# Where dS is turned and multiplied in an attention backward: fewer turns on TensorE, more products on GpSimd, dQ one group later

## The chip, the cores and the metric

The kernel runs on one core of a Trainium2 chip. The metric is the device time of one execution in microseconds, the median of several runs. PE is the matrix engine (TensorE), ACT is ScalarE, DVE is VectorE, POOL is GpSimd and SP is SyncE, which here issues DMAs.

## The reference

The program is a transformer block with adaptive layer norm, forward and backward: it returns the block's output and the gradients of nine inputs. The sequence has 2048 rows, the model 512 columns, and the attention 32 heads of 16 columns each.

```
h = layernorm(x) * (1 + ca) + sa                    # sa, ca, ga, sb, cb, gb from silu(c) @ w_mod
q, k, v = split(h @ wqkv)                           # 32 heads of 16
p = softmax(q k^T / 4);  o = p v
x = x + ga * (o @ wo)
h = layernorm(x) * (1 + cb) + sb
out = x + gb * (relu(h @ w1 + b1)^2 @ w2 + b2)
# and the vector-Jacobian product of all this with grad_out
```

The change is in the backward of the attention. For each head, with all 2048 x 2048 scores computed once more, it forms

```
P  = exp(scale * q k^T)            # row sums are folded into dO
dP = dO v^T - rowsum terms         # the terms ride along as two more rows of dO and v
dS = dP * P
dK = dS^T q;  dV = P^T dO;  dQ = dS k
```

## The kernel before

The forward takes the first part of the execution; it ends with the gradients of the feed-forward weights. Then `attn_bwd` works through 16 pairs of heads (`g`, `jp`). A pair is cut into 4 chunks `c` of 512 keys, and a chunk into 4 groups of 4 query blocks `ib` of 128 rows. A group is thus 4 blocks x 2 heads `a` = 8 tiles of 128 queries x 512 keys. I number the groups of a pair m = 0 to 15 (m = 4c + ib // 4). There are 256 groups in all.

For each tile, in the order in which the loop writes the instructions, PE computes the scores `st` (L1586), ACT takes the exponential into `pu` (L1589), and one block later PE computes `dp` (L1511, in `dP`) and DVE multiplies it with `pu` into the group's tile `ds` (L1515). Each engine runs its instructions in the written order. The PSUM tiles `st` and `dp` have three buffers each, `pu` has six, `ds` three, `dsT` four. The st and dp products use different halves of the array's rows and run side by side.

In groups with odd m (`off` is true), the second head's tile of the block i = 1 goes another way: ACT copies `dp` from PSUM to one of two SBUF tiles, `junk6` or `csq` (L1523, in `dP_pool`), and GpSimd multiplies it with `pu` (L1524). DVE has 7 products in such a group, and 8 in one with even m.

dK and dV come from `ds` and `pu` as they are (`kv`, L1455: four products side by side in four column strips of the array). `kv_two` takes two waiting units after every second block; in odd groups it takes them one at a time, at two places. dQ needs dS with the keys on the partitions. For this the group's `ds` tile, 32 blocks of 128 x 128, is transposed into `dsT` by a DMA that SP issues once a group (L1532, in `dS`), when the group's last product has been written. In groups with even m, `turn_ds` lets PE turn the first four of the blocks (L1545) into an `st` buffer, ACT copies them to `dsT` (L1546), and the DMA transposes the remaining 28. Then `dq` forms dQ (L1478) from `dsT` and the keys. Its calls wait in the list `pendq`, eight for each group; the loop takes four at every even block while more than 4 x 4 are waiting, which is to say two groups.

When a pair ends, `kvT` (filled by an ACT copy at the end of each chunk, L1458) is turned on PE and copied by ACT to `dk_t` and `dv_t` in two halves (`turn`, L1468 and L1472), and `dqT` (a DVE copy of the sums, L1483) is turned once (`turn_q`, L1491 and L1492). These three wait in `turnq`, and one is taken at block i = 3 of each group.

Loads for the next pair are cut in pieces and spread over the groups. Each is issued from GpSimd's queue (L1575) behind a copy of one element of `ds` into `tick` (L1574), which holds the load back until the group before is done.

Of the kernel before, what the change touches and what calls it, by code (L numbers as in the profile page):

```python
# [105 lines left out]
class K:  # L106
# [1322 lines left out]
    def attn_bwd(self):  # L1429
# [8 lines left out]
        S, D, H, NQ, ST, SC = self.S, self.D, self.H, self.NQ, self.ST, self.SC  # L1438
        G = 4
# [7 lines left out]
        pend, pendq, turnq = [], [], []  # L1447

        def kv(u):
            (T, g, jp, c, ib, kvT, pu, ds) = u  # L1450
            for j, (n, src) in enumerate((("Q", ds), ("dO", pu))):
                for a in range(2):
                    r = 64 * j + 32 * a
                    col = (2 * jp + a) * DH
                    nc.tensor.matmul(acckv[r:r + DH, :], lhsT=T[n][:, ib, col:col + DH], rhs=src[:, a, :],  # L1455
                                     start=(ib == 0), stop=(ib == ST - 1))
            if ib == ST - 1:
                nc.scalar.activation(kvT[:, 512 * c:512 * (c + 1)], acckv[:], ACT.Copy, scale=kvs[:])  # L1458

        def turn(g, jp, kvT, s0):  # L1460

            if kvT is None:
                return turn_q(g, jp)
            h0 = 4 * g + 2 * jp
            n = ST // 2
            tp = stp.tile([P, n, P], BF16, name="st")
            for st in range(n):
                nc.tensor.transpose(tp[:, st, :], kvT[:, (s0 + st) * P:(s0 + st + 1) * P], self.ident[:])  # L1468
            v = tp[:].rearrange("p s (t a e) -> p t s a e", t=2, a=2)
            for t, dst in enumerate((self.dk_t, self.dv_t)):  # L1470
                d = dst[:, s0:s0 + n, h0 * DH:(h0 + 2) * DH].rearrange("p s (a d) -> p s a d", a=2)
                nc.scalar.copy(d, v[:, t, :, :, 0:DH])  # L1472
# [21 lines left out]
        def kv_two(n=2):  # L1494
            for _ in range(n):
                u = pend.pop(0)
                kv(u)
                (T, g, jp, c, ib, kvT, pu, ds) = u
                if ib < ST - 1:
                    continue  # L1500
                if c % 2 and (g, jp) == (NQ - 1, 1):
                    turnq.append((g, jp, kvT, 4 * (c - 1)))
                elif c == SC - 1:
                    turnq.extend((g, jp, kvT, s0) for s0 in (0, ST // 2))

        def dP(u, a):

            (T, g, jp, c, ib, kvT, pu, dsg, i, grp) = u
            rd = slice(64 - 64 * jp, 128 - 64 * jp)
            dp = dpp.tile([P, 512], F32, name="dp")  # L1510
            nc.tensor.matmul(dp[:], lhsT=T["dOT"][rd, ib * P:(ib + 1) * P],  # L1511
                             rhs=masked["VT"][a][rd, 512 * c:512 * (c + 1)], start=True, stop=True)
            if a == 1 and i == 1 and off(c, ib):
                return dp
            nc.vector.tensor_tensor(dsg[:, i, a], dp[:], pu[:, a, :], ALU.mult)  # L1515

        def off(c, ib):
            return (c * SC + ib // G) % 2 == 1

        def dP_pool(u, dp):  # L1520
            (T, g, jp, c, ib, kvT, pu, dsg, i, grp) = u
            f = (self.junk6, self.csq)[(c * SC + ib // G) // 2 % 2]
            nc.scalar.copy(f[:], dp[:])  # L1523
            nc.gpsimd.tensor_tensor(dsg[:, i, 1], f[:], pu[:, 1, :], ALU.mult)  # L1524

        def dS(u):

            (T, g, jp, c, ib, kvT, pu, dsg, i, grp) = u
            pend.append((T, g, jp, c, ib, kvT, pu, dsg[:, i]))
            if i == G - 1:  # L1530
                dsT, n = grp
                nc.sync.dma_start_transpose(dsT[:, n:, :], dsg[:].rearrange("p i a k -> p (i a k)")[:, n * P:])  # L1532
                for a in range(2):
                    for sub in range(4):
                        pendq.append((T, g, jp, c, ib - G + 1, a, sub, dsT))

        def turn_ds(dsg, grp, skip):

            dsT = dtp.tile([P, 8 * G, P], BF16, name="dsT")
            grp.extend((dsT, 0 if skip else 4))  # L1540
            if skip:
                return
            tp = stp.tile([P, 4, P], BF16, name="st")
            for b in range(4):
                nc.tensor.transpose(tp[:, b, :], dsg[:, 0, 0, b * P:(b + 1) * P], self.ident[:])  # L1545
            nc.scalar.copy(dsT[:, 0:4, :], tp[:])  # L1546
# [4 lines left out]
        for g in range(NQ):  # L1551
            for jp in range(2):
                if jp == 0:
                    if g + 1 < NQ:
                        Tn, later = self.load_group(g + 1)
                    else:
                        Tn, later = None, self.wq_pieces(1) + self.load_wmt()
                    cut = len(later) // 2 if Tn else len(later)
                    pieces = self.pair_pieces(g, 1) + later[:cut]
                    later = later[cut:]  # L1560
                elif g + 1 < NQ:
                    pieces = self.pair_pieces(g + 1, 0) + later
                else:
                    pieces = [(self.xhat1_6[:, st, :], self.xhat1_d.rearrange("(st p) d -> p st d", p=P)[:, st, :])
                              for st in range(ST)]
                kvT = kvp.tile([P, S], BF16, name="kvT")
                total = len(pieces)
                for c in range(SC):
                    c0 = 512 * c
                    for ib0 in range(0, ST, G):  # L1570
                        m = c * (ST // G) + ib0 // G
                        while pieces and (total - len(pieces)) * SC * ST <= m * G * total:
                            if last:
                                nc.gpsimd.tensor_copy(tick[:], last[7][0:1, 0, 0, 0:1])  # L1574
                            nc.gpsimd.dma_start(*pieces.pop(0))  # L1575
                        dsg, grp = self.dsp.tile([P, G, 2, 512], BF16, name="ds"), []
                        for i in range(G):
                            ib = ib0 + i
                            q = slice(ib * P, (ib + 1) * P)
                            if turnq and i == 3:  # L1580
                                turn(*turnq.pop(0))
                            pu = self.pup.tile([P, 2, 512], BF16, name="pu")
                            for a in range(2):
                                stt = stp.tile([P, 512], F32, name="st")
                                rs = slice(64 * jp, 64 * jp + 64)
                                nc.tensor.matmul(stt[:], lhsT=T["QT"][rs, q], rhs=masked["KT"][a][rs, c0:c0 + 512],  # L1586
                                                 start=True, stop=True)
                                held = dP(last, a) if last else None
                                nc.scalar.activation(pu[:, a, :], stt[:], ACT.Exp, scale=self.scale)  # L1589
                                if held is not None:  # L1590
                                    dP_pool(last, held)
                                if a == 0 and i % 2 == 1 and off(c, ib) and len(pend) >= 4:
                                    kv_two(1)
                            if last:
                                dS(last)
                            last = (T, g, jp, c, ib, kvT, pu, dsg, i, grp)
                            if i % 2 == 1 and len(pend) >= 4:
                                kv_two(1 if off(c, ib) else 2)
                            elif i % 2 == 0 and len(pendq) > 4 * G:
                                for _ in range(8 if len(pendq) > 6 * G else 4):  # L1600
                                    dq(pendq.pop(0))
                            if i == 2:
                                turn_ds(dsg, grp, off(c, ib))
            T = Tn
        with tc.manual_schedule(engines=ALL):
            for t in (2, 0):
# [339 lines left out]
```

## Time and profile before

| | |
|---|---|
| Median of 3 runs | 2515.72 us (2510.71 to 2517.65) |
| The profiled execution | 2515.11 us, of which the span from the first to the last instruction is 2513.3 us |
| Granted TensorE clock, mean | 0.998 |
| Busy, share of the span | PE 97%, PEld 45%, DVE 68%, ACT 91%, POOL 28% |
| First and last exponential of the backward | 1166.5 and 2387.7 us |
| DMA transposes of dS | 256; 5.3 / 6.9 / 9.7 us from issue to landing (least, median, most) |
| Queue of these transposes | 71.5% of the time of 16 DMA engines |

The profile is of one execution. A line of its groups gives the source line, engine and operation, out<-in by the program's names, the shapes and the count, then the busy time and the mean duration of one in ns, then the idle time of the engine before these instructions and what ended most of it. Durations of neighbouring instructions on one engine overlap, so the distance between two starts is often less than the duration.

### The profile page before, as it was taken

What the parts mean: (1) busy time and instruction counts of PE and PEld (TensorE: products, weight loads), DVE (VectorE), ACT (ScalarE), POOL (GpSimd) and SP (SyncE); (2) the same over time, 40 slices, a digit from 0 to 9 for tenths busy, and PEclk for the clock granted to TensorE, in tenths of its full rate; (3) what the DMA queues carried; (4) which work ended last, traced back from release to release, by engine and by line L of the source; (5) the groups of instructions that cost most, each with busy time, mean ns of one, the idle gap of its engine ahead of it and who ended that gap; (6) DMA issues with size and microseconds to landing.
All of it is one profiled execution on the core that took longest, in us unless ns stands there. A gap on an engine that the chain in (4) does not pass through costs nothing.

```text
span 2513.3 us, 76903 instructions
## 1 busy us (share of the span) xinstructions
PE 2437.6 (97%) x30791; PEld 1133.6 (45%) x30791; DVE 1708.5 (68%) x3519; ACT 2297.0 (91%) x3773; POOL 715.9 (28%) x1289
## 2 busy tenths in 40 slices
PE   8999999999999999999999999999999999999998
PEld 4555555555555554673333333333333333333343
DVE  6222323422332333677999999999999999999957
ACT  7999999999999997535999999999999999999935
POOL 2344531321131022255222222222222222222223
PEclk9999999999999999999999999999999999999999
DMA  4589661441343044699999999999999999999997
GB/s 166 135 180 206 173 117 67 112 100 45 102 118 75 24 134 134 133 203 210 233 225 218 219 228 221 228 227 219 221 221 226 227 224 219 227 224 231 237 191 205
DMA packets 1260558, 446.30 MB, mean 178 GB/s; under 512 B 1204052, under 2 KB 1228246, under 8 KB 1260198
## 3 DMA queue, kind: packets, MB, share of 16 engines
q1 hardware_dynamic: 1219654, 336.29, 71.5%
q0 software_dynamic: 38464, 104.04, 13.7%
q8 instruction: 241, 3.95, 0.6%
q10 hardware_dynamic: 2080, 1.05, 0.1%
q14 instruction: 119, 0.97, 0.1%
HBM read 75.83 MB, written 64.49 MB: 56 GB/s over the span
## 4 chain that ended last, share of the span: by engine, by line
PE 55%; ACT 24%; DMA 12%; issue 4%; DVE 3%; POOL 0%; SPq 0%; DVEq 0%; ACTq 0%; POOLq 0%
ACT pu L391 19%; PE st L1586 15%; DMA dsT<-ds 10%; PE st L388 8%; PE acckv L1455 7%; PE accq L1478 5%; ACT pu L1589 4%; PE accbank L322 3%; DVE ds L1515 2%; PE dps L1050 2%; PE pps L1237 2%; PE dp L1511 1%; PE st L1545 1%; PE dps L995 1%; PE pps L631 1%
## 5 line engine op out<-in xcount | busy, mean ns | idle before, releaser
L1515 DVE TENSOR_TENSOR ds<-dp,pu 128x512 bf16<-128x512 f32 x1920 | 1180.5, 684 | 33.2 <-PE dp L1511 26.4
L1589 ACT ACTIVATE pu<-st 128x512 bf16<-128x512 f32 x2048 | 1075.3, 657 | 34.6 <-PE st L1586 21.3
L391 ACT ACTIVATE pu<-st 128x1024 bf16<-128x1024 f32 x992 | 912.1, 1077 | 2.9 <-PE st L388 2.7
L388 PE MATMUL st<-QTm,KTq 128*128 128x512 bf16 x1984 | 587.7, 377 | 19.5 <-ACT pu L391 6.0
L322 PEld LDWEIGHTS <-pu 128*128 128x128 bf16 x8192 | 347.5, 96 | 235.7 <-issue 2.5
L1511 PE MATMUL dp<-kvm,q 64*128 64x512 bf16 x1024 | 363.5, 384 | 1.3 <-DVE g2w L1056 0.7
L1511 PE MATMUL dp<-kvm,dOTg 64*128 64x512 bf16 x1024 | 362.2, 384 | 0.0
L322 PE MATMUL accbank<-Vaug,pu 128*128 128x17 bf16 x8192 | 357.7, 171 | 1.2 <-ACT Vaug L522 0.9
L1586 PE MATMUL st<-kvm,q 64*128 64x512 bf16 x1024 | 349.9, 381 | 4.7 <-ACT pu L1589 0.2
L1586 PE MATMUL st<-kvm,QTg 64*128 64x512 bf16 x1024 | 349.4, 381 | 4.0
L388 PEld LDWEIGHTS <-KTq 128*128 128x128 bf16 x1984 | 188.1, 96 | 176.1 <-issue 124.4
L1524 POOL TENSOR_TENSOR ds<-junk,pu 128x512 bf16<-128x512 f32 x64 | 73.9, 1154 | 370.3 <-ACT junk L1523 284.1
L1455 PE MATMUL acckv<-ds,Qg 128*16 128x512 bf16 x1024 | 176.2, 382 | 0.0
L1455 PE MATMUL acckv<-pu,dOg 128*16 128x512 bf16 x1024 | 175.9, 382 | 0.0
L1455 PE MATMUL acckv<-pu,q 128*16 128x512 bf16 x1024 | 175.8, 382 | 0.0
L1455 PE MATMUL acckv<-ds,q 128*16 128x512 bf16 x1024 | 175.8, 382 | 0.0
L1524 POOL TENSOR_TENSOR ds<-csq,pu 128x512 bf16<-128x512 f32 x64 | 73.8, 1153 | 354.5 <-ACT csq L1523 354.5
L302 POOL DMA_DIRECT2D QTm<-QTq_d x124 | 63.3, 512 | 340.8 <-PE st L388 320.0
L1586 PEld LDWEIGHTS <-q 64*128 64x128 bf16 x1024 | 66.9, 93 | 141.0 <-issue 108.8
L1586 PEld LDWEIGHTS <-QTg 64*128 64x128 bf16 x1024 | 66.6, 93 | 141.0 <-issue 108.0
L329 DVE RECIPROCAL rl<-accbank 128x4 f32<-128x4 f32 x128 | 23.0, 179 | 157.4 <-PE accbank L322 157.2
L1478 PE MATMUL accq<-dsT,Kg 128*32 128x128 bf16 x4096 | 105.5, 221 | 10.5 <-DMA dsT<-ds 10.2
(387 smaller groups left out, 3168.2 us busy)
## 6 DMA issues: line engine op xcount, KB each, us to landing
KTq<-KTq_d POOLq DMA_DIRECT2D x24, 512.0 KB, 3.7
duT_d<-auT POOLq DMA_DIRECT2D x3, 1792.0 KB, 7.7
aT_d<-rT POOLq DMA_DIRECT2D x3, 1792.0 KB, 11.1
KTq_d<-KTq SPq DMA_DIRECT2D x32, 128.0 KB, 2.2
QTq_d<-ev_fm SPq DMA_DIRECT2D x32, 128.0 KB, 4.3
ktm_d<-ev_tm POOLq DMA_DIRECT2D x32, 128.0 KB, 2.6
VTq_d<-vT POOLq DMA_DIRECT2D x4, 1024.0 KB, 6.3
dsT<-ds SPq DMA_TRANSPOSE x256, 6.9
```

The source lines that it names most:

```text
L302: nc.gpsimd.dma_start(QTm[j][32 * j:32 * j + 32, :], self.QTq_d[g, 32 * j:32 * j + 32, 512 * qc:512 * (qc + 1)])
L322: nc.tensor.matmul(acc[:, a, sub, :], lhsT=pu[:, a, sub * P:(sub + 1) * P], rhs=Vaug[:, kb, h, :], start=(kb == 0 and a == 0 and sub == 0) ...
L388: nc.tensor.matmul(stt[:, a, :], lhsT=KT[:, kb * P:(kb + 1) * P], rhs=QTm[2 * jp + a][:], start=True, stop=True)
L391: nc.scalar.activation(pu[:], stt[:], ACT.Exp, scale=self.scale)
L1050: nc.tensor.matmul(pt[:], lhsT=a[st], rhs=g_tm[:, st, :], start=(st == 0), stop=(st == ST - 1))
L1455: nc.tensor.matmul(acckv[r:r + DH, :], lhsT=T[n][:, ib, col:col + DH], rhs=src[:, a, :], start=(ib == 0), stop=(ib == ST - 1))
L1478: nc.tensor.matmul(accq[32 * i:32 * i + 32, ib0 // G, :], lhsT=T["K"][:, 4 * c + sub, col:col + 32], rhs=dsT[:, (i * 2 + a) * 4 + sub, :], ...
L1511: nc.tensor.matmul(dp[:], lhsT=T["dOT"][rd, ib * P:(ib + 1) * P], rhs=masked["VT"][a][rd, 512 * c:512 * (c + 1)], start=True, stop=True)
L1515: nc.vector.tensor_tensor(dsg[:, i, a], dp[:], pu[:, a, :], ALU.mult)
L1524: nc.gpsimd.tensor_tensor(dsg[:, i, 1], f[:], pu[:, 1, :], ALU.mult)
L1586: nc.tensor.matmul(stt[:], lhsT=T["QT"][rs, q], rhs=masked["KT"][a][rs, c0:c0 + 512], start=True, stop=True)
L1589: nc.scalar.activation(pu[:, a, :], stt[:], ACT.Exp, scale=self.scale)
```

## The change

There are four edits, all in `attn_bwd`.

- `turn_ds` skips all groups but the first of each chunk: PE turns four blocks in m = 0, 4, 8, 12. In all other groups the DMA transposes all 32 blocks.
- GpSimd's product is also used in m = 6, 10 and 14, so in eleven groups of a pair. The buffer for it is chosen by the parity of m. Whether `kv_two` is split still depends on the parity of m alone.
- dQ waits until more than six times four calls are waiting, which is three groups; in the last pair it stays at two.
- The turns of dK and dV are taken from m = 2 on, and that of dQ from m = 7 on.

```diff
+        def odd(c, ib):
+            return (c * SC + ib // G) % 2 == 1
+
+        def no_turn(c, ib):
+            return ib // G > 0
+
         def off(c, ib):
-            return (c * SC + ib // G) % 2 == 1
+            return odd(c, ib) or (c and ib // G == 2)
...
-            f = (self.junk6, self.csq)[(c * SC + ib // G) // 2 % 2]
+            f = (self.junk6, self.csq)[(c * SC + ib // G) % 2]
...
+                lag = 4 if (g, jp) == (NQ - 1, 1) else 6
...
-                            if turnq and i == 3:
+                            if turnq and i == 3 and m >= (7 if turnq[0][2] is None else 2):
                                 turn(*turnq.pop(0))
...
-                                if a == 0 and i % 2 == 1 and off(c, ib) and len(pend) >= 4:
+                                if a == 0 and i % 2 == 1 and odd(c, ib) and len(pend) >= 4:
                                     kv_two(1)
...
-                                kv_two(1 if off(c, ib) else 2)
-                            elif i % 2 == 0 and len(pendq) > 4 * G:
-                                for _ in range(8 if len(pendq) > 6 * G else 4):
+                                kv_two(1 if odd(c, ib) else 2)
+                            elif i % 2 == 0 and len(pendq) > lag * G:
+                                for _ in range(8 if len(pendq) > (lag + 2) * G else 4):
                                     dq(pendq.pop(0))
                             if i == 2:
-                                turn_ds(dsg, grp, off(c, ib))
+                                turn_ds(dsg, grp, no_turn(c, ib))
```

## The prediction

> **What bounds the kernel now.** The only stretch that the change touches is the attention backward, from the first exponential at 1166 us to the last at 2388 us: 256 groups (16 pairs of heads x 16 groups), 4.77 us a group, 76.4 us a pair. I read the page's groups first, for what one group consists of.
>
> ```profile
> L1515 DVE TENSOR_TENSOR ds<-dp,pu 128x512 bf16<-128x512 f32 x1920 | 1180.5, 684 | 33.2 <-PE dp L1511 26.4
> L1589 ACT ACTIVATE pu<-st 128x512 bf16<-128x512 f32 x2048 | 1075.3, 657 | 34.6 <-PE st L1586 21.3
> L1524 POOL TENSOR_TENSOR ds<-junk,pu 128x512 bf16<-128x512 f32 x64 | 73.9, 1154 | 370.3 <-ACT junk L1523 284.1
> L1478 PE MATMUL accq<-dsT,Kg 128*32 128x128 bf16 x4096 | 105.5, 221 | 10.5 <-DMA dsT<-ds 10.2
> ```
>
> Then the stretch by windows of 100 us (columns: us, then busy us with count for PE, PEld, DVE, ACT, POOL; clock, DMA share, GB/s): ACT over 99%, PE and DVE over 97%, no throttling.
>
> ```profile
> 1500.00:1600.00 100.00, 98.70 (x1418) 36.41 (x1416) 98.41 (x161) 99.66 (x203) 27.44 (x55) 1.00 1.16 224
> 1600.00:1700.00 100.00, 98.34 (x1424) 36.11 (x1424) 98.00 (x161) 99.40 (x202) 26.37 (x53) 1.00 1.18 226
> ```
>
> Records of one engine overlap and stretch, so a busy share near one does not tell which engine is the bound. The spacing of starts does. The timeline of ACT and then of DVE at the start of a pair:
>
> ```profile
> 1702.91 1.12 ACT L1589 ACTIVATE pu<-st 128x512 bf16<-128x512 f32 x2
> 1703.87 0.72 ACT L1458 ACTIVATE kvT<-acckv,kvs 128x512 bf16<-128x512 f32 x1
> 1704.44 3.09 ACT L1589 ACTIVATE pu<-st 128x512 bf16<-128x512 f32 x6
> 1707.31 0.71 ACT L1523 COPY junk<-dp 128x512 f32<-128x512 f32 x1
> 1707.78 0.52 ACT L1472 COPY dk_t<-st 128x256 bf16<-128x256 bf16 x1
> 1708.04 0.53 ACT L1472 COPY dv_t<-st 128x256 bf16<-128x256 bf16 x1
> 1708.30 4.20 ACT L1589 ACTIVATE pu<-st 128x512 bf16<-128x512 f32 x8
> ```
> ```profile
> 1712.81 0.68 DVE L1483 TENSOR_SCALAR dqT<-accq 128x512 bf16<-128x512 f32 x1
> 1713.41 4.27 DVE L1515 TENSOR_TENSOR ds<-dp,pu 128x512 bf16<-128x512 f32 x7
> 1718.04 1.34 DVE L1515 TENSOR_TENSOR ds<-dp,pu 128x512 bf16<-128x512 f32 x2 [0.36 <-PE dp L1511]
> ```
>
> Six exponentials from 1704.44 to 1707.31 are 0.478 us each (0.477 is the least over all), a copy of 512 columns 0.47, a kvT copy 0.57, a dk/dv couple 0.53, a dq copy 0.48. DVE's seven products are 0.598 each ((4.27 - 0.08)/7), dqT 0.60. So a pair is at the least: ACT 128 x 0.477 + 16 x 0.466 + 4 x 0.57 + 2 x 0.53 + 0.48 = 72.3 us; DVE 121 x 0.598 = 72.4. PE, from the least spacing of its blocks in the timeline (four st/dp products 0.535, or 0.319 for two; kv 0.54 for two units, 0.325 for one; 16 dQ products 0.34; four turning products 0.33), is 8 x 4.23 + 8 x 4.32 + 1.4 for the turns = 69.8. **Three engines are within 4% of each other and lose 4 us a pair to one another**, and which is the bound changes inside the pair. Group period by its number m in the pair (starts of the exponentials, mean of the pairs), two groups together because the three PSUM buffers of st and of dp smooth only a group or so:
>
> m: 0+1 10.16; 2+3 10.13; 4+5 9.31; 6+7 9.25; 8+9 9.46; 10+11 9.39; 12+13 9.56; 14+15 9.10.
> ACT least: 9.66; 9.57; 9.13; 8.56; 9.13; 8.56; 9.13; 8.56 (8.56 = 16 x 0.477 + 2 x 0.466, plus what the pair's start and the kvT copies add).
> DVE least: 8.97 each (15 x 0.598), 9.57 with dqT in m = 3.
>
> The larger of the two sums to 73.53, the measured to 76.36: 2.83 us a pair are lost to PE and its waits. The wait view says what PE waits for: "PE accq L1478 <- DMA dsT<-ds: 15.1, 29, 1.3", that is 15 us in 29 waits, 1.0 us a pair.
>
> **What the Trainium skill says.** "ScalarE: Activation LUTs", What ACT_TABLE_LOAD costs: 186 ns + 0.833 ns an element with immediates, back to back overlapping by 93 ns, so an estimate of 0.52 us here; the trace shows 0.477 and decides. "SBUF — State Buffer", SBUF: two separate sides: GpSimd and DVE share a port pair, for a DVE product only with two SBUF inputs; here one input is PSUM, so no full block is due. The trace agrees, with a remainder: DVE's spacing beside a GpSimd product is 0.644 in the median instead of 0.598. "DMA: Bandwidth & Descriptors", Latency and other measured facts: 261 GB/s for a DMA transpose; 32 blocks of 32 KB at that rate are 4.0 us, and the shortest of 32 blocks here is 3.98.
>
> **The change, part by part.**
>
> 1. TensorE turns in m = 0, 4, 8, 12 alone (from m = 0, 2, ..., 14). A pair loses 4 x 0.33 = 1.32 us of PE, four ACT copies (4 x 0.466 = 1.86) and four uses of an st buffer. Four transposes a pair grow from 28 blocks to 32.
> 2. GpSimd takes the product in m = 6, 10, 14 too. DVE loses 3 x 0.598 = 1.79 us a pair, less 3 x 2 x 0.046 where GpSimd overlaps; ACT gains 3 x 0.466 = 1.40; POOL gains 3 x 1.15 = 3.5 us, at 28% busy. On POOL the product stands between the load of its group and the tick of the next, which waits for DVE anyway. The acckv product that reads its tile comes over 2 us after the dp tile, and 0.47 + 1.15 cover it: cost nothing, or 0.5 us a product if kv must wait (0 to 24 us in all; I take 0). The two buffers: csq is used again two groups (9 us) later at the least.
> 3. The two kv turns move from m = 1, 2 to m = 2, 3, the dq turn from m = 3 to m = 7: no work saved, but ACT's load is levelled.
> 4. dQ runs three groups behind instead of two (not in the last pair). dQ starts 2.37 us after the last packet in the mean, the landing is told 1.3 us after that packet; 4.7 us more lets every DMA wait go. What is late next is the ds buffer: it has three, DVE's first write for group m + 3 comes 3.55 us (least 2.1) after the last packet of m, so 2.2 us after landing. dsT has four buffers; its last reader in m + 4 stands before the new writer on PE, so no new wait.
>
> The least sums after, in the same columns. ACT: 9.13; 9.15; 9.13; 9.04; 9.13; 8.56; 9.13; 8.56. DVE: 8.97; 9.57; 8.97; 8.37; 8.97; 8.37; 8.97; 8.37. The larger sum to 72.25: **1.28 us a pair less**. Of the 2.83 us lost, I take 0.55 of the 0.97 us of DMA waits as regained (ACT's lookahead hid the rest; bounds 0 and 1.0), 0.2 for the room on PE (0 to 0.8), and give 0.3 back for longer transposes (0 to 2). Together 1.7 us a pair.
>
> 5. The transposes' own stream. On SP a DMA_TRANSPOSE lasts 4.47 us in the mean with 32 blocks and 4.04 with 28 (least 3.98 and 3.43), with 0.09 between. A pair is 8 x 4.47 + 8 x 4.04 + 1.4 = 69.5 us now; after, 12 x 4.47 + 4 x 4.04 + 1.4 = 71.2 of some 74.7: 95% full. In the last two pairs, where weights and xhat load at 131 to 197 KB a group instead of some 66, back-to-back transposes already take 4.65 to 5.26; there I expect no gain.
>
> Sum: 14 x 1.7 = 24 us. The profiled execution took 2515.1 (span 2513.3, 1.8 around it), the median is 2515.7: **2491.5 us**. Everything before 1166 and after 2388 stays.
>
> **Rivals.**
>
> A. The DMA becomes the bound; slower. The mechanism: SP falls behind, a ds buffer lands late, and DVE's first product of a group waits for the transpose of three groups before. It decides where the sustained time of a transpose passes 4.77 us, today's group; between 4.65 and 4.77 it eats the gain. For it: eight groups that ran back to back (from 1439.6 us) took 4.70 each with half of them at 32 blocks; a quarter more at +0.43 gives 4.81, so 256 x 0.04 = +10 us: 2526. Against: other such runs moved on at 4.05 to 4.5 between last packets, and the mean of all, gaps included, is 4.34.
>
> B. ACT is the sole bound, as its 99% suggests. Then only its one copy less counts: 16 x 0.466 = 7.5 us: 2508. Against: ACT loses 65 us in the stretch to starts spaced over their least, nearly all behind PE.
>
> C. PE's room closes most of what is lost: half of the 2.83 goes too, 2.7 us a pair: 16 x 2.7 = 43: 2472.
>
> D. The change doesn't do what it says: the built program has one transpose of 28 blocks, then three of 32, throughout, and the ACT copies as described. No chance given.
>
> **How the numbers follow.** The likeliest (2478 to 2502) has 0.55, C 0.15, B (2502 to 2512) 0.15, A 0.15, half of it slower. A change under 0.3% (7.5 us, about what a measurement of this kernel can tell from none) is "same". Faster: 0.55 + 0.15 + 0.11 of B = 0.81. Slower: 0.08. Same: 0.11. The range, 2470 to 2511, leaves out A's slower part and the far end of C.
>
> **What would show it.** Right: the accq wait on dsT falls from 15 us to under 4; L1515's product count 1872 (was 1920) and GpSimd's 176; m = 6+7 and 10+11 nearest to ACT's 9.04 and 8.56; m = 0+1 about half a microsecond shorter. Wrong: DVE ds waiting for DMA dsT by over 10 us in all, or SP transposes back to back throughout (A); all two-group periods as before but for 0.06 (B); a period over 76.4.

## The result, and the profile after

The changed kernel is slower: median 2538.73 us against 2515.72, ratio 1.0091 with a 95% interval of 1.0076 to 1.0107. Its profiled execution took 2538.31 us, with a span of 2536.5. The stretch of the backward, first to last exponential, grew from 1221.3 to 1246.8 us, so the loss lies there. The forecast was 2491.5 us, with the sign the other way; the rival A (2526 us) is the one that came true, and more strongly than it was worked out.

A part of that growth is this one execution's. In the changed kernel's profile the granted TensorE clock is halved five times inside the stretch, for 20.4 us in all; in the profile of before it is never below 1.00 there. Two of these places, in the last two pairs, in the windows view (us, busy us of PE, PEld, DVE, ACT and POOL, then the clock):

```profile
2309.80:2313.20 3.40, 3.40 (x36) 0.72 (x32) 2.77 (x6) 2.57 (x5) 1.14 (x3) 0.50 1.40 286
2330.30:2337.10 6.80, 6.80 (x66) 1.85 (x60) 4.28 (x7) 3.82 (x7) 1.97 (x4) 0.50 1.24 278
```

My estimate is that TensorE loses half of that time by it, 10 us where the stretch grew by 25.5; what the whole kernel loses can be less or more. It does not explain the change: the five executions have mean clocks of 0.994 to 0.997, and the two at 0.997 took 2538.7 and 2540.9 us, while 19 executions of the kernel before at 0.997 (on the chip of e9 to e12) took 2517.2 in the mean.

The page's groups of the changed kernel (line, engine, operation; busy us and mean ns; idle us before it, and what ended it):

```profile
L1515 DVE TENSOR_TENSOR ds<-dp,pu 128x512 bf16<-128x512 f32 x1872 | 1164.5, 683 | 73.8 <-DMA dsT<-ds 29.5
L1596 ACT ACTIVATE pu<-st 128x512 bf16<-128x512 f32 x2048 | 1075.0, 655 | 40.9 <-PE st L1593 23.4
...
L1511 PE MATMUL dp<-kvm,dOTg 64*128 64x512 bf16 x1024 | 370.6, 388 | 14.1 <-DVE ds L1515 13.5
```

The counts are those of the forecast (1872 products on DVE). But DVE's idle time rose from 33 to 74 us, and the name behind most of the rise is new: the transpose of dS. PE in turn waits for DVE before dp (before: 0.0).

The same two windows as before, of the changed kernel:

```profile
1500.00:1600.00 100.00, 98.01 (x1390) 34.75 (x1386) 95.91 (x155) 98.92 (x201) 31.00 (x57) 1.00 1.28 229
1600.00:1700.00 100.00, 96.48 (x1355) 33.13 (x1354) 93.29 (x151) 96.69 (x194) 30.90 (x57) 1.00 1.27 224
```

All three compute engines are less busy than before, and the DMA share is higher (1.28 and 1.27 for 1.16 and 1.18). No engine became busier, which points to something outside them. The waits of DVE and PE inside the stretch, changed kernel:

```profile
DVE ds L1515 <- DMA dsT<-ds: 29.5, 38, 1.8
PE dp L1511 <- DVE ds L1515: 25.8, 40, 1.7
PE accq L1478 <- DMA dsT<-ds: 2.2, 2, 1.9
```

The dQ wait fell from 15.1 us to 2.2, as forecast. In its place stand 38 waits of DVE for a transpose that has still to free its ds buffer. The tile view of ds for the transposes (least, median and most ns on SP; then us to landing), of the kernel before:

```profile
L1532 SPq DMA_TRANSPOSE dsT<-ds x256: 3433/4162/6181, 1173.0 to 2389.8; - x128
...
DMA to landing us min/median/max: 5.3/6.9/9.7
```

and of the changed kernel:

```profile
L1538 SPq DMA_TRANSPOSE dsT<-ds x256: 3527/4511/6605, 1173.5 to 2416.8; - x128
...
DMA to landing us min/median/max: 5.9/7.8/11.1
```

Taken one by one, the changed kernel's transposes follow each other with no more than 0.12 us between in 206 of 255 cases; before it was 64. Their lengths sum to 1201 us of the 1243 us from the first issue to the last (1090 of 1217 before). One place shows how a late transpose spreads. First DVE's timeline in the changed kernel, then ACT's:

```profile
1643.83 2.58 DVE L1515 TENSOR_TENSOR ds<-dp,pu 128x512 bf16<-128x512 f32 x4
1647.50 9.27 DVE L1515 TENSOR_TENSOR ds<-dp,pu 128x512 bf16<-128x512 f32 x15 [1.09 <-DMA dsT<-ds]
1657.03 6.39 DVE L1515 TENSOR_TENSOR ds<-dp,pu 128x512 bf16<-128x512 f32 x10 [0.26 <-DMA dsT<-ds]
```
```profile
1644.09 4.13 ACT L1596 ACTIVATE pu<-st 128x512 bf16<-128x512 f32 x8
1649.32 0.59 ACT L1552 COPY dsT<-st 128x512 bf16<-128x512 bf16 x1 [1.10 <-PE st L1551]
1649.80 1.09 ACT L1596 ACTIVATE pu<-st 128x512 bf16<-128x512 f32 x2
```

DVE cannot write the first tile of its new group until 1647.50. TensorE's turn of that tile is late by as much, and ACT, which runs in order, stands 1.10 us before the copy of the turned blocks, with its exponentials queued behind.

### The profile page after: what moved, and what is told of

Same layout as the page of the kernel before. It is cut to its first block, busy times and chain, and to the rows that moved or that the text cites. A ratio compares the mean times of both kernels' runs of the same rounds, so it can differ in the third digit from the quotient of the medians.

```text
span 2536.5 us, 76311 instructions
## 1 busy us (share of the span) xinstructions
PE 2448.3 (97%) x30535; PEld 1109.6 (44%) x30535; DVE 1693.8 (67%) x3471; ACT 2298.4 (91%) x3757; POOL 766.3 (30%) x1337
## 3 DMA queue, kind: packets, MB, share of 16 engines
q1 hardware_dynamic: 1252422, 344.68, 74.6%
## 4 chain that ended last, share of the span: by engine, by line
PE 53%; ACT 25%; DMA 14%; issue 4%; DVE 3%; POOL 1%; SPq 0%; DVEq 0%; ACTq 0%; POOLq 0%
ACT pu L391 18%; PE st L1593 13%; DMA dsT<-ds 12%; PE st L388 8%; PE acckv L1455 6%; ACT pu L1596 5%; PE accq L1478 4%; PE accbank L322 3%; PE dp L1511 2%; DVE ds L1515 2%; PE dps L1050 2%; PE pps L1237 2%; PE dps L995 1%; PE dp L1646 1%; PE pps L631 1%
## 5 line engine op out<-in xcount | busy, mean ns | idle before, releaser
L1515 DVE TENSOR_TENSOR ds<-dp,pu 128x512 bf16<-128x512 f32 x1872 | 1164.5, 683 | 73.8 <-DMA dsT<-ds 29.5
L1511 PE MATMUL dp<-kvm,dOTg 64*128 64x512 bf16 x1024 | 370.6, 388 | 14.1 <-DVE ds L1515 13.5
L1593 PE MATMUL st<-kvm,q 64*128 64x512 bf16 x1024 | 344.1, 382 | 3.7 <-ACT pu L1596 0.2
L1530 POOL TENSOR_TENSOR ds<-csq,pu 128x512 bf16<-128x512 f32 x128 | 147.2, 1150 | 605.5 <-ACT csq L1529 464.5
L1478 PEld LDWEIGHTS <-Kg 128*32 128x32 bf16 x4096 | 60.8, 96 | 116.8 <-issue 116.6
L1478 PEld LDWEIGHTS <-keep 128*32 128x32 bf16 x4096 | 59.5, 95 | 114.3 <-issue 114.3
```

The costliest lines, as they stand in the source:

```text
L1478: nc.tensor.matmul(accq[32 * i:32 * i + 32, ib0 // G, :], lhsT=T["K"][:, 4 * c + sub, col:col + 32], rhs=dsT[:, (i * 2 + a) * 4 + sub, :], ...
```

## The experiments

Four edits make up the change. The runs undo or do them singly, cut the DMA's work, and try to win. Each ratio is to the kernel before on the same chip. "Back to back" counts the transposes that follow the one before by at most 0.12 us; it and the time of a pair come from one profiled execution of each kernel. e3, e4 and e10 do not compute all of the gradients: e3 forms a part of dQ from other blocks, e4 and e10 leave out the loads of twelve pairs.

| Kernel | Median us | Ratio to before, 95% | Back to back | Pair, us (pairs 0 to 13) |
|---|---|---|---|---|
| before | 2515.7 | 1 | 64 | 76.1 |
| changed | 2538.7 | 1.0091 (1.0076 to 1.0107) | 206 | 77.2 |
| e1, turns of dS undone | 2521.6 | 1.0019 (1.0008 to 1.0031) | 88 | 76.7 |
| e2, turns of dS alone | 2536.6 | 1.0074 (1.0047 to 1.0101) | 113 | 77.4 |
| e3, changed with 28 blocks a transpose | 2488.5 | 0.9894 (0.9871 to 0.9916) | 29 | 74.6 |
| e4, changed without loads in 12 pairs | 2505.1 | 0.9956 (0.9941 to 0.9971) | 95 | 74.8 |
| e5, later dQ alone | 2528.8 | 1.0034 (1.0021 to 1.0047) | 108 | 76.7 |
| e6, later dQ and moved turns | 2532.7 | 1.0051 (1.0034 to 1.0068) | 160 | 77.2 |
| e7, GpSimd's eleven alone | 2526.5 | 1.0028 (1.0018 to 1.0038) | 56 | 77.1 |
| e8, changed with four ds buffers | 2530.3 | 1.0040 (1.0026 to 1.0055) | 115 | 77.0 |
| e9, moved turns alone | 2518.4 | 1.0006 (0.9993 to 1.0018) | 67 | 76.2 |
| e10, e6 without loads in 12 pairs | 2510.7 | 0.9971 (0.9953 to 0.9989) | 61 | 75.5 |
| e11, dQ half a group later, moved turns | 2526.8 | 1.0045 (1.0028 to 1.0061) | 134 | 77.0 |
| e12, turned blocks copied on DVE | 2519.5 | 1.0003 (0.9993 to 1.0013) | 81 | 76.6 |

In some profiles a pair contains 3.4 or 6.8 us at half the TensorE clock. Without such pairs the last column reads 77.1 for the changed kernel, e1 76.5, e2 77.1, e6 76.8, e7 76.9, e8 76.9, e11 76.7 and e12 76.5; the others have none among pairs 0 to 13.

### e1: the turns of dS undone

```diff
         def no_turn(c, ib):
-            return ib // G > 0
+            return odd(c, ib)
```

> The changed kernel with one part undone: TensorE again turns four blocks in eight groups of a pair (every even m), so the transposes are 28 blocks in eight groups and 32 in eight; GpSimd's eleven products, the later dQ and the moved turns stay. Theory V (the transposes' volume is the bound: four more transposes of 32 blocks filled the DMA): the transposes no longer run back to back, DVE's waits for a transpose to free a ds buffer fall from 29.5 us to under 5, and the time is below the kernel before, some 2500 us (2490 to 2512): ACT and DVE floors as before, less the dQ waits. Theory G (GpSimd's products, or the later dQ with its older buffers, cost the time; the turns are innocent): stays near 2538 us or gets worse by the 64 PE turns and ACT copies given back.

Measured: 1.0019 of before. DVE's wait for the transposes is 4.3 us in 7 waits, and 88 transposes are back to back. So with the turns undone most of the loss is gone: this part carries it. But the gain of the forecast did not come, and at 1.0019 it is still a little slower than before: the other three parts together bring none.

### e2: the turns of dS alone

```diff
-                                turn_ds(dsg, grp, off(c, ib))
+                                turn_ds(dsg, grp, ib // G > 0)
```

> The kernel before with the turns' part alone: PE turns in four groups of a pair, the DMA takes 32 blocks in twelve; dQ stays two groups behind, GpSimd has eight products. Theory V: slower than the kernel before by as much as the change or more, 2535 to 2560 us, transposes back to back, and here the waits stand at dQ (accq for dsT well over the 15 us of before), since dQ comes a group earlier. Theory G: 2515 us or a little faster, since PE and ACT have less to do.

Measured: 1.0074, 19 us, on a kernel that has less work on PE and on ACT. The wait is where theory V put it, at dQ; the wait view of e2:

```profile
PE accq L1478 <- DMA dsT<-ds: 35.7, 60, 2.0
```

Sixty waits in place of 29. Where the wait stands depends on the lag of dQ: here PE waits, in the changed kernel DVE. The other half of the forecast did not hold: only 113 transposes are back to back. In pairs 0 to 13 they take 4.55 us with 32 blocks and 4.28 with 28, which is 12 x 4.55 + 4 x 4.28 = 71.7 us of the 77.4 of a pair. So a transpose can be late for dQ although the queue has room in the mean.

### e3: less volume, all else equal

```diff
-            grp.extend((dsT, 0 if skip else 4))
+            grp.extend((dsT, 4))
...
-                                 rhs=dsT[:, (i * 2 + a) * 4 + sub, :],
+                                 rhs=dsT[:, ((i * 2 + a) * 4 or late4) + sub, :],
```

`late4` is 8 where PE turned none, and 0 elsewhere.

> The changed kernel with the DMA's volume cut and nothing else: each transpose takes 28 blocks, also in the twelve groups in which TensorE turns none; dQ then reads another four blocks of the group in place of the four that are left out, so part of dQ is computed from other data. PE, ACT, DVE and GpSimd have exactly the work of the changed kernel. Theory V: the gain that the accounting of ACT, DVE and PE promised appears, 2480 to 2500 us, and SP has gaps between transposes again. Theory G: stays near 2538 us.

Measured: 2488.5 us. This is the decisive run: the engines' work and its order are those of the changed kernel, and 48 blocks a pair fewer on the DMA (448 for 496) turn 0.9% slower into 1.1% faster. What the 1.1% owes to the engines' part of the change stays open, for 448 is also less than the 480 of the kernel before, and no run gives that kernel the same cut. Its waits, tile view and windows:

```profile
DVE ds L1517 <- PE dp L1513: 11.2, 36, 0.7
PE dp L1513 <- DVE ds L1517: 0.7, 3, 0.3
PE accq L1480 <- DMA dsT<-ds: 0.5, 1, 0.5
```
```profile
L1540 SPq DMA_TRANSPOSE dsT<-ds x256: 3413/3708/5517, 1176.5 to 2366.6; - x128
```
```profile
1500.00:1600.00 100.00, 98.94 (x1421) 35.96 (x1420) 97.59 (x158) 100.00 (x204) 32.66 (x60) 1.00 1.13 213
1600.00:1700.00 100.00, 99.07 (x1424) 35.86 (x1422) 97.79 (x159) 99.93 (x204) 29.89 (x57) 1.00 1.10 215
```

Of the waits for a transpose one of 0.5 us is left, ACT is busy for practically all of both windows, and the pairs take 74.6 us, nearly all alike.

### e4: no loads beside the transposes

```diff
-                            nc.gpsimd.dma_start(*pieces.pop(0))
+                            piece = pieces.pop(0)
+                            if g in (0, NQ - 1):
+                                nc.gpsimd.dma_start(*piece)
```

> The changed kernel without the loads of the middle twelve pairs (the tick copies stay; those pairs compute with the operands of the first ones, so their gradients are others). The transposes keep their volume, but have the 16 DMA engines for themselves. Theory V in the form that the sum of transposes and loads fills the DMA engines: a transpose of 32 blocks falls from 4.8 towards 4.0 us in those pairs, their period falls from 77.3 us on average to some 74.7, 2505 us in all (2495 to 2515). Theory S (the transposes alone, at the rate at which SP issues them, are the bound, and the loads don't matter): no change, 2535 us. Theory G: no change.

Measured: 2505.1 us, and 74.6 to 74.8 us in each of the twelve pairs. In these pairs a transpose of 32 blocks takes 4.31 us in the mean, and 4.85 in the same pairs of the changed kernel. So it is transposes and loads together that cost the time; the transposes at their full volume of 496 blocks fit when they are alone. Theory S is out. GpSimd's issuing of these loads is gone too, but e3 keeps it and has no loss.

### e5 and e6: the later dQ, alone and with the moved turns

```diff
+                lag = 4 if (g, jp) == (NQ - 1, 1) else 6
...
-                            elif i % 2 == 0 and len(pendq) > 4 * G:
-                                for _ in range(8 if len(pendq) > 6 * G else 4):
+                            elif i % 2 == 0 and len(pendq) > lag * G:
+                                for _ in range(8 if len(pendq) > (lag + 2) * G else 4):
```

> The kernel before with the later dQ alone (three groups behind, two in the last pair). Theory V: the 15 us of dQ waits for a transpose go, but for the last pair; ACT's lookahead had hidden some, so 5 to 12 us faster than before, 2504 to 2511 us; DVE waits for ds buffers stay under 5 us, since the transposes still have their gaps. Theory L (the later dQ itself costs, since it keeps dsT and its sums longer): 2516 us or more.

Measured: 1.0034, slower. Two lines of its wait view:

```profile
PE st L1491 <- DVE dqT L1483: 15.2, 14, 1.1
PE accq L1478 <- DMA dsT<-ds: 3.8, 5, 1.2
```

Most of the dQ wait is gone, and an equal one has come: the last dQ of a pair now falls in the very group whose turn of dQ follows it, and PE stands 1.1 us a pair until DVE has copied the sums. That is what the moved turns avoid. e6 adds them:

```diff
-                            if turnq and i == 3:
+                            if turnq and i == 3 and m >= (7 if turnq[0][2] is None else 2):
```

> The kernel before with the later dQ and the moved turns of dK, dV (from m = 2) and dQ (from m = 7), but its own eight turns of dS and its eight GpSimd products. By the floors the moved turns save 0.4 us a pair beside what the later dQ saves: 2495 to 2506 us, and faster than both kernels. If the moved turns bring nothing: as the kernel with the later dQ alone.

Measured: 1.0051, still slower, though the wait for dqT is gone. Pairs 7 to 10 take 75.3 us, close to what its accounting promised (76.1 less 0.4 for the moved turns and 0.55 for dQ's waits); the others go up to 78.9, and to 81.8 and 80.8 in pairs 3 and 14, in which the clock is halved for 3.4 us. The volume of transposes is that of the kernel before, yet 160 are back to back, and DVE waits:

```profile
DVE ds L1515 <- DMA dsT<-ds: 12.6, 15, 2.2
```

Pair 7 has no transpose back to back and a mean length of 4.06 us; pair 4, at 78.6 us, has all 16 and 4.85. Back to back alone is no loss: pair 10 has 10 of them, at a mean of 4.51 us, and takes 75.3.

### e7: GpSimd's eleven products alone

```diff
         def no_turn(c, ib):
-            return ib // G > 0
+            return odd(c, ib)
...
-                lag = 4 if (g, jp) == (NQ - 1, 1) else 6
+                lag = 4
```

and the turn times of before; all from the changed kernel.

> The kernel before with GpSimd's eleven products alone (TensorE turns in eight groups, dQ two groups behind, the turns at their old places). By the floors ACT gets 3 x 0.466 = 1.4 us a pair more, where the larger floor of groups 6+7, 10+11 and 14+15 rises from DVE's 8.97 to ACT's 9.03, so 0.2 us a pair: 2512 to 2525 us. If GpSimd's products beside DVE cost more than that (DVE's spacing of 0.644 in place of 0.598, ds tiles ready later): over 2530 us.

Measured: 2526.5 us, 1.5 us over the upper end. The loss stands in groups 6+7, 10+11 and 14+15 (9.53, 9.56 and 9.57 us without pair 0, in which the clock is halved; before 9.27, 9.30 and 9.09), where ACT has both a turned copy and a GpSimd copy in one group; ACT's floor there is 4.75 us for the even group and 4.28 for the odd one, and the queue of three buffers does not seem to smooth it as I had assumed; this is read from the floors and not tested. In e3, whose groups 6, 10 and 14 have only the GpSimd copy, the same three take 9.43, 9.04 and 9.04. So it seems that GpSimd's products can pay only together with the turns that are taken away.

### e8: a fourth ds buffer

```diff
-        self.dsp = self.open_pool("p5ds", bufs=3)
-        self.dtp = self.open_pool("p5dt", bufs=4)
+        self.dsp = self.open_pool("p5ds", bufs=4)
+        self.dtp = self.open_pool("p5dt", bufs=3)
...
-                lag = 4 if (g, jp) == (NQ - 1, 1) else 6
+                lag = 4
```

> The changed kernel with four ds buffers in place of three, for which dsT has three in place of four and dQ goes back to two groups behind (there is no room for both). Theory V, in the form that the rate of the DMA engines is the bound: another buffer moves the wait but takes none away; the transposes stay back to back and the time 2530 to 2550 us, with the wait at dQ or SP. Theory B (the DMA keeps up in the mean and only the ds buffer comes free too late): DVE's wait for a transpose goes and the time falls well below the 2537 us of the turns alone, to 2515 us or less.

Measured: 2530.3 us. DVE waits for no transpose any more, and dQ does:

```profile
PE accq L1478 <- DMA dsT<-ds: 40.9, 64, 2.1
```

The wait moved and did not go. 115 transposes are back to back and not 206, since waits at dQ hold up the whole loop, DVE included; the part of theory V that said they stay back to back did not hold. In pairs 0 to 13 they take 4.60 and 4.17 us. That the kernel is faster than the changed one (1.0040 for 1.0091) can be the lag or the buffer; the run cannot tell these apart.

### e9 to e12: who keeps the DMA in step, and can it be won

e9 is the kernel before with the moved turns alone (the diff of e6's second edit).

> The kernel before with only the turns of dK, dV (from m = 2) and dQ (from m = 7) moved. By the floors groups 0+1 fall from 9.66 to 9.13, 2+3 rise from 9.57 to 9.62: 0.4 us a pair, 6 us in all, 2505 to 2516 us. Theory R (what is saved on the engines in this kernel is lost again to the transposes' queue, because groups that come faster leave it no gaps): the same time as before or slower, with more transposes back to back than the 64 of before.

Measured: 1.0006, no difference. Groups 0+1 fell from 10.12 to 9.66 us, nearly by what the floors said, and 2+3 and 6+7 rose to 10.29 and 9.73.

e10 is e6 with e4's edit.

> The kernel with the later dQ and the moved turns (eight turns, eight GpSimd products, the volume of transposes of before) without the loads of the middle twelve pairs, which so compute with the operands of the first ones. Theory R: it was slow because its transposes run back to back; without loads its twelve pairs take the 75.3 us that its four quiet pairs already took, and the time is 2533 - 12 x 1.9 = 2510 us (2500 to 2514). If the later dQ costs by itself (another wait, dsT held longer): 2525 us or more.

Measured: 2510.7 us, and 75.3 to 75.4 us in each of the twelve pairs. So the later dQ shows no cost of its own when there are no loads beside the transposes. What the kernel before would take without these loads was not run, so this is no proof of a gain by the later dQ. The tile view of e10:

```profile
L1532 SPq DMA_TRANSPOSE dsT<-ds x256: 3399/4000/6037, 1173.5 to 2382.7; - x128
```

e11 is e6 with `lag` 5 in place of 6.

> The same kernel with the loads, and with dQ half a group later than before in place of a whole one. Theory R, in the form that dQ's waits for a transpose are the brake that keeps DMA and engines in step: between the kernel with the turn times alone and the one a whole group later, 2512 to 2530 us, back-to-back transposes between 64 and 160. If the half group already ends the waits and the queue keeps its gaps: 2500 to 2508 us.

Measured: 2526.8 us with 134 back to back. With the same turns moved, the median goes 2518.4, 2526.8, 2532.7 as dQ comes 0, 1/2 and 1 group later, and the back-to-back count 67, 134, 160 (e9 to e11 and e6 ran on two chips, whose kernels before stand at 2517.1 and 2518.4). The intervals of the last two overlap, so only the step from e9 to the others is clear. I read it so: freeing PE of its wait brings the groups closer, and the transposes lose the gaps in which they caught up.

e12 is e7 with the moved turns, and

```diff
-            nc.scalar.copy(dsT[:, 0:4, :], tp[:])
+            (nc.vector.tensor_copy if on_dve else nc.scalar.copy)(dsT[:, 0:4, :], tp[:])
```

where `on_dve` is true for turned blocks in m = 6, 10 and 14.

> A version meant to be faster than both: eight turns of dS (volume of transposes as before), GpSimd's eleven products, dQ two groups behind, turns of dK, dV and dQ moved, and in m = 6, 10, 14 the copy of the turned blocks on DVE, which GpSimd has relieved there. Floors: 9.13, 9.62, 9.13, 9.04, 9.13, 8.73, 9.13, 8.73 = 72.6 us a pair in place of 73.5: 14 us, 2502 us, if the transposes' queue lets it. Theory R: it does not, since at some 75.4 us a pair the queue is full at 480 blocks too: 2510 to 2520 us.

Measured: 1.0003. The 14 us of the floors did not come; dQ waits 22.5 us for transposes in place of 15.1. No version that computes everything beat the kernel before.

## Why the prediction was wrong

**Right, as far as it was tested: the engines' sum.** The accounting of ACT and DVE by two groups, with 1.7 us a pair to be gained, agrees with e3 and e4, where the DMA has room: 74.6 us a pair, which is the 76.36 of the prediction less 1.7. How much of this comes from the engines and how much from the freer DMA these runs do not part; e3 has no dQ waits at all, of which the sum took only a half as regained. Groups 6+7, 10+11 and 14+15 stand in e3 at 9.43, 9.04 and 9.04, some 0.4 over ACT's 9.04 and 8.56.

**Right in kind: step 4.** The dQ wait went (15.1 to 2.2 us), and what is late next is the ds buffer, as written. The size was off: its margin after the last packet fell from 3.55 to 2.52 us, with 0.64 at the least, and the landing is told 1.55 us after the packet.

**The step that failed is step 5, and with it the 0.3 us a pair that the sum gave back for longer transposes.** By the distance from e3 to the changed kernel, 77.2 for 74.6, that term was 2.6 us, outside its bounds of 0 to 2. Step 5 took the mean lengths of the transposes, 4.47 and 4.04 us, from a stretch in which they had gaps, as what they would take without gaps: 71.2 us of 74.7, 95% full. In the same pairs of the changed kernel (0 to 13) they take 4.83 and 4.21, so 12 x 4.83 + 4 x 4.21 + 1.4 = 76.2 us: more than the 74.7 that the engines would need, and nearly the 77.2 of a pair. The evidence lay beside it: the eight back-to-back transposes at 4.70, from which rival A worked out 4.81. The measured group is 77.2 / 16 = 4.83. I gave that rival 0.15 because other runs of transposes moved on at 4.05 to 4.5 us between last packets. Four runs of four transposes give these figures, three intervals each, counted from the last packet of the first; from start to start on SP the same runs went on at 4.77 to 5.19 us, so they were no evidence against A.

The sum of 76.2 us is of the changed kernel alone. e2 and e8 have the same 496 blocks, and their transposes fill 72 and 72 of 77 us a pair, yet they lose 0.7% and 0.4%. There single late transposes hold up dQ; the common cause that e3 and e4 show is the volume beside the loads, and a full queue is one form of the loss.

**Rival A's size.** It had 10 us. Fourteen pairs lost 1.15 us each against before, which is 16; the other 9 came from the last two pairs, 165.9 us for 156.5, where I expected no gain but no loss either. In 17 of these us the clock was halved, which can be most of it in this execution (TensorE loses 8.5 us by it, an estimate); e1, e2, e5 and e9, with no such place there, take 155 to 158. How the loss divides in the other executions is not known.

**The 0.55 us a pair for dQ's waits** were no gain to be had in this kernel. e6 and e11 show that ending them without giving the DMA room makes the kernel slower, and e10 that without loads it does not. My reading is that what these waits bought was time for the transposes.

**The signs named in the prediction**: accq under 4 us (2.2, right), the counts (right), groups 0+1 half a microsecond shorter (9.78 for 10.12 over the same 14 pairs, two thirds of it), 6+7 and 10+11 nearest to ACT's floor (9.87 and 9.29, wrong), and of the signs of being wrong, DVE waiting over 10 us for transposes, the mark of A (29.5), and a period over 76.4 (77.2).

What stays open is why transposes in a full queue take longer than the same ones with gaps: with 32 blocks 4.89 us back to back and 4.56 after a gap in the changed kernel, while before it was 4.46 and 4.43, and in e2 and e8, with the same volume as changed, 4.62 and 4.61 back to back and 4.50 and 4.60 after a gap. So being back to back does not lengthen them by itself. A part can be read below; no run here isolates it.

## What to carry to other kernels

A queue that is kept busy 90% of the time is a bound in waiting: do not price work that is moved onto it by the mean length of items among gaps (4.47 us here became 4.83), and ask whether the wait that an edit removes was what gave it those gaps. Before work goes from busy engines to the DMA, cut the DMA's volume by a trial as in e3: it tells in one run whether the transfer is what costs. Give the kernel before the same cut as well, which was not done here, and the difference is the engines' side alone. Of an edit in several parts, those that can only pay together (here perhaps GpSimd's products with the turns taken away, and the later dQ with the moved turns) do not show their worth when tried singly. And look at the clock of each pair before you compare pairs of two profiles.

## What the runs showed of the hardware

**Transposes that meet an instruction fetch are longer.** In the kernel before the instruction queue moves a packet of 16 KB every 9.1 us, about every second group, and the packet keeps one DMA engine for 1.08 us. I count a transpose as meeting it when the packet starts between 0.3 us after the transpose's issue and 0.4 us after the end of its record on SP; pairs 0 to 13. In the kernel before, a 32-block transpose that met such a packet took 4.84 us in the mean (43 of them), one that met none 4.19 (69); in the changed kernel 5.24 (80) and 4.45 (88). In e3, with 28 blocks, 4.25 (66) and 3.68 (158). Counted by any overlap with the record the difference is smaller but stays: 4.66 and 4.18 before, 5.22 and 4.41 in the changed kernel. Those that met none are longer in the changed kernel too, so fetches are not the whole of it. This is read from coincidence in time; the fetches were not varied.

**The clock is halved for a few microseconds at a time.** In the profiles of the changed kernel, e1, e2, e4, e6 to e8 and e10 to e12 it falls to 0.50 inside the stretch for 3.4 or 6.8 us at a time, one to five times, and in those of before, e3, e5 and e9 never. A pair among 0 to 13 that contains such a place is 1.1 to 5.0 us longer than the mean of the others of its kernel. The spread between executions goes with it: of the kernel before on the chip of e9 to e12, five at a mean clock of 0.999 took 2514.2 us in the mean, 19 at 0.997 2517.2 and 8 at 0.996 2522.1. What sets off these places the runs do not show.

**The rate of the transposes.** The 261 GB/s that the Trainium skill states for a DMA transpose ("DMA: Bandwidth & Descriptors", Latency and other measured facts; for a non-contiguous middle dimension, with some 350 to 400 for the contiguous case) lead to an estimate of 4.0 us for 32 blocks. The shortest are 3.98 in the kernel before and 3.84 in e10, which is 273 GB/s; no run comes near 350. But beside loads and fetches the changed kernel's stream goes on at 31 blocks in 4.83 us, which is 31 x 32.8 KB / 4.83 us = 210 GB/s. The measured rate decides what the queue can hold.
